# First block's operand sums made in later blocks from reloaded quadrants, six raw weight tiles at the start, a later slot for the key maxima, and later reuse of seven rooms

## The chip, the cores and the metric

The kernel runs on one core of a Trainium2 chip. The metric is device time in microseconds of one execution. Three runs of the kernel before gave 1580.91, 1583.93 and 1583.86 us, a median of 1583.86 us. The profiled execution is another one and took 1588.23 us.

## What is computed

Inputs `q`, `k`, `v` have 8 batches, 8 heads, 576 positions and 64 features. `q` is turned into a softmax over the features, `k` into a softmax over the positions. Then, for each batch and head, `kv = k_s^T v` (64 x 64) and `x = q_s kv`, and the heads are laid side by side: `x` is 4608 x 512. Two two-layer networks follow:

```python
h = x @ w_in          # 512 -> 2048
g = relu(h) ** 2
x = g @ w_out         # 2048 -> 512
h2 = x @ w_in2        # 512 -> 2048
g2 = h2 * sigmoid(h2)
out = g2 @ w_out2     # 2048 -> 512
```

The four weight matrices are handed over as 64-bit floats.

## The kernel before, in words

**Precision.** A matmul operand is split into a high part that TensorE takes at its fast rate and a low part; each product is three matmuls, high by high, high by low and low by high. So every weight and every activation costs a cast on ACT and a subtraction on DVE.

**Weights.** A weight tile comes as pairs of 32-bit words (`raw_load`, L166, 512 KB, a tile `wraw`). `rounding` (L198) makes 32-bit floats of it: a copy of the low words on ACT and three operations on DVE (`wu`). `w1_split` (L245) then makes `wh` on ACT and `wl` on DVE. The 16 tiles of the first layer (`wlist`, L1013) use three buffers, `doubles` (L118). The first three loads stand among the loads of the first inputs (`first_loads`, L1020); the other 13 are issued in the first seven slots of block 0, each when a buffer is free (L1117 to L1124).

**First stage.** The tokens are taken in nine blocks of 512 (L1096). A block has 16 slots; in slot t the matmul group `layer_in` (L673, 12 matmuls into bank `h`) makes 128 hidden features for the block's 512 tokens, and `hidden` (L694) squares the positive part on ACT into a tile `gs`. The attention of the next block is spread over the same slots: the table `ORDER` (L727) gives each step (`kv_max`, `kv_tr`, `kv_red`, `kv_diag`, `kv_bc`, `kv_sub`, `kv_exp`, `kv_mm`, ...) its slot, and `at` (L723) files it. From block 1 on every engine runs its instructions in the order of the program (`pinned`, L1099); in block 0 the compiler's scheduler chooses the order.

**Quadrants.** The later layers multiply 2 x 2 block matrices with seven products instead of eight. That needs, besides the four quadrants A11, A12, A21, A22 of an activation, the sums S1 to S4, where S3 takes the place of A21. In the first stage `g_first` (L705) makes S1 and S3 on DVE, `g_second` (L710) makes S2 and S4 on POOL, and `g_store` (L715) writes all seven slots of 128 x 256 to DRAM (`g1d`, 896 KB) from POOL's queue. A pair j of hidden tiles is written in slots 2j and 2j+1, summed in slots 2j+3 and 2j+4 and stored in slot 2j+5. `g_place` (L690) gives each pair one of six places: three tiles of 7 x 512, of which two are the tiles `st` of `stpool` and the third lies in `gpool`.

**After the first stage.** Steps (L771) take products one after another. Each step needs a pair `al`, `ah` of the activation (`a_load` on SP's queue 14 steps ahead, L778, `a_split` six steps ahead, L791) and a split weight (`product_weights`, L334). All of these live in rooms of 128 x 512 (`room`, L122), taken from the front of the queue `rooms` and given back at its end. When the first stage ends, `gpool` is closed, a pool `rpool` takes its bytes and 13 rooms are appended (L1143 to L1145). The two tiles `st` become slots for results, from which `hidden_after` (L864) takes its first two, `c11`, after the eighth step.

Of the kernel before, what the change touches and what calls it, by code (L numbers as in the profile page):

```python
# [10 lines left out]
I32 = mybir.dt.int32  # L11
# [14 lines left out]
def kernel(  # L26
# [36 lines left out]
    class InOrder:  # L63
# [16 lines left out]
    ve, ac, gp, sp, pe = (  # L80
        InOrder(e) for e in (nc.vector, nc.scalar, nc.gpsimd, nc.sync, nc.tensor)
    )
    P = 128
# [4 lines left out]
    TB = P * R  # L88
    HB = TB // 2
    NB = NT // TB  # L90
    KC = DM // P
    NF = DFF // P
    NG = NF // 2
# [20 lines left out]
    NU = 76  # L114

    rooms, banks, a_banks = deque(range(NU)), deque((0, 1, 6)), deque((2, 3, 4, 5, 7))
    lent, rpool = {}, []
    doubles = deque(range(3))  # L118
    g_pool_was = tc.tile_pool(name="gpool", bufs=1)
    g_pool = g_pool_was.__enter__()  # L120

    def room(dt=F32, name="u"):  # L122
        n = rooms.popleft()
        t = (upool if n < NU else rpool[0]).tile([P, TB], dt, tag=f"u{n}", name=name)
        lent[id(t)] = (t, n, rooms)
        return t
# [7 lines left out]
    def back(*ts):  # L134
        for t in ts:
            _, n, whence = lent.pop(id(t))
            whence.append(n)
# [14 lines left out]
    g1d = [dpool.tile([P, 7, NB * HB], F32, name=f"g1d{j}") for j in range(NG)]  # L152
    wd = {(ph, f): dpool.tile([P, DM], F32, name=f"wd{ph}_{f}") for ph in (1, 2, 3) for f in range(NF)}

    S2, S1, A21, A11, A22, A12, S4 = range(7)
    S3 = A21

    PRODUCTS = (
# [7 lines left out]
    def raw_load(ph, f):  # L166

        if ph < 2:
            n = doubles.popleft()
            t = g_pool.tile([P, 2 * TB], I32, tag=f"d{n}", name="wraw")  # L170
            lent[id(t)] = (t, n, doubles)
            if ph:
                src = w_out[ph].bitcast(I32)[f * P:(f + 1) * P, :]
            else:
                src = w_in[ph].bitcast(I32)[:, 2 * f * P:2 * (f + 1) * P].rearrange(
                    "(c p) f -> p c f", p=P
                )
            sp.dma_start(out=t if ph else t.rearrange("p (c f) -> p c f", c=KC), in_=src)
            return [t]
        got = []  # L180
        for h in range(2):
            t = room(I32, "wraw")
            if ph in w_in:
                sp.dma_start(
                    out=t.rearrange("p (c f) -> p c f", c=2),
                    in_=w_in[ph].bitcast(I32)[
                        2 * h * P:2 * (h + 1) * P, 2 * f * P:2 * (f + 1) * P
                    ].rearrange("(c p) f -> p c f", p=P),
                )
            else:  # L190
                sp.dma_start(
                    out=t,
                    in_=w_out[ph].bitcast(I32)[f * P:(f + 1) * P, h * TB:(h + 1) * TB],
                )
            got.append(t)
        return got
# [42 lines left out]
    def w1_load(x):  # L239
        raw1[x] = raw_load(*x)  # L240

    def w1_round(x):
        raw1[x] = rounded(x[0], raw1[x])
# [443 lines left out]
    g_tiles = [stpool.tile([P, 7, TB], F32, tag="st", name="gs") for _ in range(2)]  # L687
    g_tiles.append(g_pool.tile([P, 7, TB], F32, tag="gs", name="gs"))

    def g_place(i, j):  # L690
        n = i * NG + j
        return g_tiles[n // 2 % 3][:, :, n % 2 * HB:(n % 2 + 1) * HB]

    def hidden(i, f, h):  # L694
# [18 lines left out]
        gp.tensor_tensor(t[:, S4], t[:, A12], t[:, S2], op=ALU.subtract)  # L713

    def g_store(i, j):  # L715
        gp.dma_start(
            out=g1d[j][:, :, i * HB:(i + 1) * HB], in_=g_place(i, j)
        )


    side = {}

    def at(i, slot, fn, *a):  # L723
        i, slot = divmod(max(0, i * NF + slot), NF)
        side.setdefault((i, slot), []).append((fn, a))

    ORDER = (  # L727
        (x_mm, 12), (kv_mm, 4), (kv_tr, 0), (kv_red, 1), (q_out, 6), (q_back, 8),
        (kv_load, -5), (q_load, -3), (v_load, 0),
        (kv_max, -1), (kv_sub, 2), (kv_exp, 3), (kv_rc, 5),  # L730
        (kv_scale, 6), (kv_lo, 7), (q_max, 1), (q_sub, 2), (q_exp, 3), (q_norm, 4), (q_tr, 5),
        (q_hi, 10), (q_lo, 11), (x_hi, 13), (x_lo, 14), (kv_diag, 1), (kv_bc, 1),
    )
    OF_KV = (kv_load, v_load, kv_max, kv_tr, kv_bc, kv_diag, kv_red, kv_sub, kv_exp, kv_mm, kv_rc, kv_scale, kv_lo)
    for i in range(NB):
        for j in range(NG):
            at(i, 2 * j + 3, g_first, i, j)
            at(i, 2 * j + 4, g_second, i, j)
            at(i, 2 * j + 5, g_store, i, j)
    early = []  # L740
    for fn, d in ORDER:
        for nxt in range(1, NB):
# [270 lines left out]
    wlist = [(0, f) for f in FS]  # L1013
# [3 lines left out]
        qmax=q_max, qsub=q_sub, qexp=q_exp, qnorm=q_norm, qtr=q_tr, qout=q_out, qhi=q_hi, qlo=q_lo, kvmm=kv_mm,  # L1017
        rc=kv_rc, scale=kv_scale, xmm=x_mm, xhi=x_hi, xlo=x_lo, round=w1_round, split=w1_split,
    )
    first_loads = "q0 v0 w0 q1 k1 v1 q2 k2 v2 w1 q3 k3 v3 w2".split()  # L1020
    whole = "kmax kred qmax qsub qexp ksub kexp qnorm kvmm qtr qout rc scale qhi qlo xmm xhi xlo".split()
    first_steps = [f"{x}{j}" for j in range(KC) for x in whole]
    for x, before in (("round0", "qnorm0"), ("split0", "rc0"), ("round1", "kmax3"), ("split1", "kvmm3")):
# [39 lines left out]
    def go_on():  # L1063

        doing[:] = [x for x in doing if next(x, 0) != 0]
# [26 lines left out]
    nl = sum(what[0] == "w" for what in first_loads)  # L1092
# [3 lines left out]
    for n in range(NB * NF + 6):  # L1096
        i, t = divmod(n, NF)
        ends = i >= NB - 1
        pinned[0] = i > 0  # L1099
        if n == (NB - 1) * NF:  # L1100
            assert nw == len(w2list)
            back(kv_room, *kv_rooms, *kvf_rooms.values())
            todo = [(5, lambda g=g: raw_weights(1, g)) for g in range(NG)]
            todo += [
                (NG if m in (3, 2, 1, 5) else 0, lambda m=m: product_weights(1, m)) for m in FIRST_USE
            ]
        last = hs
        if n < NB * NF:
            f = FS[t]
            hs = i, f, layer_in(i, f)  # L1110
            if ends:
                back(wh1.pop((0, f)), wl1.pop((0, f)))
        else:
            hs = None
        if last:
            hidden(*last)
        for _ in range(2):  # L1117
            if i == 0 and nr < len(wlist):
                if nl < len(wlist):
                    w1_load(wlist[nl])  # L1120
                    nl += 1
                w1_round(wlist[nr])
                w1_split(wlist[nr])
                nr += 1  # L1124
        for fn, a in side.pop((i, t), ()):
            fn(*a)
        if not ends:
            go_on()
            if n >= 33 and nw < len(w2list) and t in (1, 4, 7):
                doing.append(round_to_dram(*w2list[nw]))  # L1130
                next(doing[-1])
                nw += 1
        elif n < NB * NF:
            if t >= 9:
                stream(2 * t - 32)
                stream(2 * t - 31)
            for _ in range(3):
                spare = 2 + AHEAD + SPLIT - held_by(1) - 2 * (NF - 1 - t)
                while todo and len(doing) < 6 and len(rooms) - owed[0] >= todo[0][0] + max(0, spare):
                    begin()  # L1140
                go_on()
    assert not side
    g_pool_was.__exit__(None, None, None)  # L1143
    rpool.append(ctx.enter_context(tc.tile_pool(name="rpool", bufs=1)))
    rooms.extend(range(NU, NU + 13))  # L1145
    banks.extend(a_banks)

    st.update({e: stpool.tile([P, 7, TB], F32, tag="st", name="st") for e in range(2)})
# [6 lines left out]
    ROUNDS |= {(2, u, x) for u in range(NS - 1) for x in (14, 24, 34)}  # L1155
    for n, (ph, u, x, j, done) in enumerate(steps):
        into = n % SUPER
        if into == 0:
            if done and ph == 1:
                todo += [(8, lambda g=g: seven(2, g)) for g in range(NG)]  # L1160
                todo[4:4] = [(4, lambda m=m: factor(0, m)) for m in FIRST_USE]
            if done and ph == 2:
                todo += [(5, lambda g=g: raw_weights(3, g)) for g in range(NG)]
                todo += [
                    (NG if m in (3, 2, 1, 5) else 0, lambda m=m: product_weights(3, m))
                    for m in FIRST_USE[:5] + (6, 5)
                ]
            if ph == 3 and u == ORDER3[0]:
                back(extra)
        if ph == 2 and not done and (x, j) == (0, NG - 2):  # L1170
            todo += [(4, lambda m=m, u=u: factor(u + 1, m)) for m in FIRST_USE]
        if w3list and (ph, u, into) in ROUNDS:
            doing.append(round_to_dram(*w3list.pop(0)))
            next(doing[-1])
        if ph == 2:
            catch_up(lambda: (2, j, x) in W and ready((2, u, x, 0)) and ready((2, u, x, 1)))
        else:
            catch_up(lambda: (ph, j, x) in W)
        stream(n)
        step(ph, u, x, j, done)  # L1180
        go_on()
        if ph == 2:
            spare = 2 if done else 0
        else:
            left = sum(m[0] == ph for m in steps[n + 1:n + 1 + AHEAD])
            spare = 2 + left + min(left, SPLIT) - held_by(ph)
        many = 7 if ph == 2 and not done else 5 if ph == 1 and done else 2
        while todo and len(doing) < many and len(rooms) - owed[0] >= todo[0][0] + spare:
            begin()
# [33 lines left out]
```

## Time and profile before

| What | us |
|---|---|
| Median of three runs | 1583.86 |
| Profiled execution | 1588.23 |
| Its span, first to last instruction | 1586.5 |
| TensorE (PE) busy | 1538.9 |
| VectorE (DVE) busy | 1122.5 |
| ScalarE (ACT) busy | 907.5 |
| GpSimd (POOL) busy | 622.0 |

All lines of the kernel's instructions are L73, a helper that records every operation, so instructions are told apart by the names of their tiles. The profiled execution lies 4.4 us above the median; its span leaves 1.7 us outside.

### The profile page before, as it was taken

The numbers are of one execution on the slowest core, as the hardware profiler recorded it, in microseconds if no ns is written. First come the engines' busy times: TensorE is split into PE (matmuls) and PEld (weight loads), VectorE is DVE, ScalarE is ACT, GpSimd is POOL, SyncE is SP. The second block draws the span as 40 slices with busy tenths as digits, with TensorE's granted clock in tenths as the row PEclk, the third lists the DMA queues.
The fourth block names the chain that finished last, engine by engine and source line by source line (L and its number), as shares of the span: only waits on it lengthen the run. The fifth ranks groups of instructions, "written<-read, shape, count | busy, mean of one in ns | idle before, by whom it ended". The sixth has DMA issues, their size and how long they took to land.

```text
span 1586.5 us, 25384 instructions
## 1 busy us (share of the span) xinstructions
PE 1538.9 (97%) x7676; PEld 1332.5 (84%) x7676; DVE 1122.5 (71%) x2260; ACT 907.5 (57%) x1926; POOL 622.0 (39%) x1009
## 2 busy tenths in 40 slices
PE   5979999999999899999999999999999999999998
PEld 3758888888888799999988999999988899888997
DVE  7996778887626876777698866766666965655654
ACT  6856666666545755455567554645555845444441
POOL 1054455555548210202042744444467140606150
PEclk9989999999999999999999999999999999999999
DMA  9668899998867788989897687778789786867682
GB/s 251 198 216 253 290 289 288 298 297 266 269 223 226 269 274 297 310 282 326 275 335 245 226 298 255 273 246 300 261 300 317 259 246 198 249 190 235 190 275 47
DMA packets 264713, 410.15 MB, mean 259 GB/s; under 512 B 70272, under 2 KB 199296, under 8 KB 264576
## 3 DMA queue, kind: packets, MB, share of 16 engines
q1 hardware_dynamic: 210896, 238.23, 49.0%
q0 software_dynamic: 50272, 168.86, 29.7%
q10 hardware_dynamic: 3408, 1.44, 0.4%
q8 instruction: 60, 0.98, 0.3%
q14 instruction: 77, 0.63, 0.1%
HBM read 230.42 MB, written 178.00 MB: 257 GB/s over the span
## 4 chain that ended last, share of the span: by engine, by line
PE 89%; DVE 3%; DMA 3%; POOL 2%; ACT 1%; issue 1%; SPq 0%; ACTq 0%; POOLq 0%; DVEq 0%
PE x L73 35%; PE h L73 23%; PE d L73 18%; PE a L73 9%; PE kvps L73 2%; PE xps L73 2%; POOL g2d L73 1%; POOL wt L73 1%; DMA al<-x2d 1%; DMA kr<-in_k_dram 1%; DVE xr L73 1%; DVE wu L73 1%; DMA wraw<-in_moe_w_in_dram 1%; DVE wl L73 0%; DMA g1d<-gs 0%
## 5 line engine op out<-in xcount | busy, mean ns | idle before, releaser
L73 DVE TENSOR_TENSOR al<-al,ah 128x448 fp32r<-128x448 f32 (+1 forms) x630 | 374.2, 642 | 188.0 <-ACT ah L73 183.6
L73 ACT CAST ah<-al 128x448 fp32r<-128x448 f32 (+1 forms) x630 | 334.4, 577 | 141.7 <-PE x L73 55.5
L73 PE MATMUL h<-x,wh 128*128 128x512 f32 x1152 | 369.3, 401 | 2.1 <-DVE x L73 1.8
L73 PE MATMUL x<-ah,wT 128*128 128x448 f32 (+1 forms) x960 | 288.4, 371 | 0.5 <-ACT st L73 0.5
L73 PEld LDWEIGHTS h<-x,wh 128*128 128x128 f32 x1152 | 216.1, 191 | 46.7 <-DVE x L73 2.0
L73 ACT COPY st<-x 128x448 f32<-128x448 f32 (+1 forms) x181 | 97.8, 543 | 251.0 <-PE x L73 236.0
L73 PE MATMUL h<-x,wl 128*128 128x512 f32 x576 | 227.3, 395 | 0.0
L73 PEld LDWEIGHTS x<-ah,wT 128*128 128x128 f32 x960 | 180.3, 188 | 21.7 <-ACT st L73 1.6
L73 POOL DMA_DIRECT2D g2d<-st x262 | 140.6, 541 | 131.5 <-ACT st L73 72.7
L73 PE MATMUL x<-al,wT 128*128 128x448 f32 (+1 forms) x480 | 178.0, 371 | 0.0
L73 POOL TENSOR_TENSOR gs<-gs 128x256 f32<-128x256 f32 x144 | 125.6, 872 | 131.5 <-DVE gs L73 102.7
L73 POOL DMA_DIRECT2D out_dram<-st x176 | 92.2, 533 | 195.8 <-DVE st L73 190.1
L73 ACT ACTIVATE gs<-h 128x512 f32<-128x512 f32 x144 | 85.8, 596 | 134.8 <-PE h L73 131.0
L73 PE MATMUL a<-ah,wB 128*128 128x448 f32 (+1 forms) x480 | 148.8, 371 | 0.0
L73 PE MATMUL d<-ah,wT 128*128 128x448 f32 (+1 forms) x480 | 145.3, 374 | 3.4 <-ACT ah L73 3.4
L73 PE MATMUL d<-ah,wB 128*128 128x448 f32 (+1 forms) x480 | 144.1, 371 | 0.0
L73 PE MATMUL x<-ah,wN 128*128 128x448 f32 (+1 forms) x480 | 143.9, 371 | 0.0
L73 PE MATMUL x<-ah,wB 128*128 128x448 f32 (+1 forms) x480 | 143.9, 371 | 0.0
L73 PEld LDWEIGHTS h<-x,wl 128*128 128x128 f32 x576 | 109.4, 190 | 24.0 <-DVE wu L73 0.2
L73 DVE TENSOR_TENSOR st<-st 128x448 f32<-128x448 f32 (+1 forms) x161 | 100.2, 648 | 26.6 <-ACT st L73 23.0
L73 PEld LDWEIGHTS d<-ah,wT 128*128 128x128 f32 x480 | 91.0, 190 | 13.7 <-issue 3.8
L73 PEld LDWEIGHTS d<-ah,wB 128*128 128x128 f32 x480 | 90.1, 188 | 10.3 <-DVE st L73 0.3
(124 smaller groups left out, 2678.9 us busy)
## 6 DMA issues: line engine op xcount, KB each, us to landing
g1d<-gs POOLq DMA_DIRECT2D x72, 896.0 KB, 5.6
al<-g1d SPq DMA_DIRECT2D x224, 224.0 KB, 4.1
al<-g2d SPq DMA_DIRECT2D x224, 224.0 KB, 3.1
g2d<-st POOLq DMA_DIRECT2D x210, 224.0 KB, 3.4
al<-g1d SPq DMA_DIRECT2D x56, 256.0 KB, 4.1
al<-g2d SPq DMA_DIRECT2D x56, 256.0 KB, 3.0
g2d<-st POOLq DMA_DIRECT2D x52, 256.0 KB, 3.9
al<-x2d SPq DMA_DIRECT2D x56, 224.0 KB, 5.4
```

The lines of the kernel that those rows point to most:

```text
L73: got = fn(*a, **kw)
```

## The change

The sums of block 0 are taken out of block 0: there `g_store` writes the four quadrants alone, two slots earlier. Each of the eight pairs is loaded again in a later block (`g_again`, `AGAIN`), summed there and its four sums are stored; blocks 1, 2, 3, 5, 6 and 7 take one pair each and block 4 takes two. The order of slots is changed so that the four sums and the four quadrants are each contiguous. Three more raw weight tiles lie in the third tile `gs` until the stage needs it (`views`; each is used twice), and three more loads stand at the end of `first_loads`, while `w1` stands ahead of the loads of head pair 2. `kv_bc`, `kv_sub`, `kv_exp`, `kv_mm`, `kv_rc`, `kv_scale` and `kv_lo` are one slot later. Of the 13 rooms, six are appended at the end of the first stage and seven at step 12. With eight more turns, the last two pairs of the stage lie in a tile `st` instead of the tile in `gpool`.

```diff
-    doubles = deque(range(3))
+    doubles, views = deque((-1, -2, -3, 0, 1, 2)), [0] * 3
...
-    S2, S1, A21, A11, A22, A12, S4 = range(7)
+    S4, S2, S1, A21, A11, A22, A12 = range(7)
...
             n = doubles.popleft()
-            t = g_pool.tile([P, 2 * TB], I32, tag=f"d{n}", name="wraw")
-            lent[id(t)] = (t, n, doubles)
+            if n < 0:
+                t = g_tiles[2].rearrange("p s c -> p (s c)").bitcast(I32)[:, 2 * TB * ~n:2 * TB * -n]
+                lent[id(t)] = (t, n, doubles if views else [])
+                views[:1] = []
+            else:
+                t = g_pool.tile([P, 2 * TB], I32, tag=f"d{n}", name="wraw")
+                lent[id(t)] = (t, n, doubles)
...
+    AGAIN = {(i, 3): i - 1 for i in (1, 2, 3, 5, 6, 7)} | {(4, 1): 3, (4, 5): 7}
+    turns = []
+    for i in range(NB):
+        for j in range(NG):
+            turns.append((i, j))
+            if (i, j) in AGAIN:
+                turns.append(AGAIN[i, j])
     def g_place(i, j):
-        n = i * NG + j
+        n = turns.index(j if i is None else (i, j))
...
     def g_store(i, j):
+        o = slice(A21, 7) if i == 0 else slice(0, A21 + 1) if i is None else slice(0, 7)
+        b = i or 0
         gp.dma_start(
-            out=g1d[j][:, :, i * HB:(i + 1) * HB], in_=g_place(i, j)
+            out=g1d[j][:, o, b * HB:(b + 1) * HB], in_=g_place(i, j)[:, o]
         )
+    def g_again(j):
+        sp.dma_start(out=g_place(None, j)[:, A21:7], in_=g1d[j][:, A21:7, 0:HB])
...
-        (x_mm, 12), (kv_mm, 4), (kv_tr, 0), (kv_red, 1), (q_out, 6), (q_back, 8),
+        (x_mm, 12), (kv_mm, 5), (kv_bc, 2), (kv_tr, 0), (kv_red, 1), (q_out, 6), (q_back, 8),
...
-        (kv_max, -1), (kv_sub, 2), (kv_exp, 3), (kv_rc, 5),
-        (kv_scale, 6), (kv_lo, 7), (q_max, 1), (q_sub, 2), (q_exp, 3), (q_norm, 4), (q_tr, 5),
-        (q_hi, 10), (q_lo, 11), (x_hi, 13), (x_lo, 14), (kv_diag, 1), (kv_bc, 1),
+        (kv_max, -1), (kv_sub, 3), (kv_exp, 4), (kv_rc, 6),
+        (kv_scale, 7), (kv_lo, 8), (q_max, 1), (q_sub, 2), (q_exp, 3), (q_norm, 4), (q_tr, 5),
+        (q_hi, 10), (q_lo, 11), (x_hi, 13), (x_lo, 14), (kv_diag, 1),
...
-            at(i, 2 * j + 3, g_first, i, j)
-            at(i, 2 * j + 4, g_second, i, j)
-            at(i, 2 * j + 5, g_store, i, j)
+            if i:
+                at(i, 2 * j + 3, g_first, i, j)
+                at(i, 2 * j + 4, g_second, i, j)
+            at(i, 2 * j + (5 if i else 3), g_store, i, j)
+            if (i, j) in AGAIN:
+                again = AGAIN[i, j]
+                at(i, 2 * j + 2, g_again, again)
+                at(i, 2 * j + 5, g_first, None, again)
+                at(i, 2 * j + 6, g_second, None, again)
+                at(i, 2 * j + 7, g_store, None, again)
...
-    first_loads = "q0 v0 w0 q1 k1 v1 q2 k2 v2 w1 q3 k3 v3 w2".split()
+    first_loads = "q0 v0 w0 q1 k1 v1 w1 q2 k2 v2 q3 k3 v3 w2 w3 w4 w5".split()
...
-                if nl < len(wlist):
+                if nl < len(wlist) and doubles:
...
-    rooms.extend(range(NU, NU + 13))
+    rooms.extend(range(NU + 7, NU + 13))
...
+        if n == 12:
+            rooms.extend(range(NU, NU + 7))
```

## Rows read from the trace of the kernel before

**Rows 1.** The page: the span, and busy time of each engine.

```profile
span 1586.5 us, 25384 instructions
PE 1538.9 (97%) x7676; PEld 1332.5 (84%) x7676; DVE 1122.5 (71%) x2260; ACT 907.5 (57%) x1926; POOL 622.0 (39%) x1009
```

**Rows 2.** The chain that ended last, first stage: start, length, what.

```profile
72.75 8.07 DMA wraw<-in_moe_w_in_dram
...
148.76 8.21 PE h L73 x36
...
161.64 8.21 PE h L73 x36
```

**Rows 3.** By stretch, blocks 4 and 5: PE, PEld, DVE, ACT, POOL, clock, DMA, GB/s.

```profile
269.50:321.00 51.50, 51.50 (x297) 41.78 (x297) 41.59 (x98) 35.03 (x72) 27.49 (x41) 1.00 0.93 297
...
324.00:337.00 13.00, 13.00 (x76) 10.54 (x75) 9.79 (x24) 8.94 (x18) 6.53 (x10) 1.00 1.02 328
```

**Rows 4.** By stretch, tile `h` alone: PE, PEld, ACT, clock, DMA, GB/s.

```profile
0.00:47.00 47.00, 8.71 (x24) 4.50 (x24) 0.00 (x0) 1.00 0.87 214
0.00:118.50 118.50, 59.21 (x205) 39.83 (x206) 9.93 (x17) 0.94 0.78 221
```

**Rows 5.** Busy time by stretch, 20 to 120 us (columns as in rows 3).

```profile
20.00:40.00 20.00, 17.04 (x104) 10.49 (x103) 15.83 (x43) 14.57 (x51) 0.87 (x1) 1.00 1.01 244
40.00:60.00 20.00, 17.08 (x134) 13.12 (x134) 18.25 (x46) 19.70 (x59) 0.29 (x3) 0.91 0.40 121
...
80.00:100.00 20.00, 15.79 (x74) 11.65 (x74) 17.46 (x35) 13.47 (x26) 8.93 (x13) 0.91 0.51 156
100.00:120.00 20.00, 13.61 (x78) 9.53 (x79) 19.45 (x49) 10.10 (x23) 12.82 (x19) 0.79 0.84 271
```

**Rows 6.** Waits of SP's queue, 0 to 125 us: total, times, longest.

```profile
SPq L73 <- DVE wu L73: 37.2, 11, 9.8
```

**Rows 7.** The end of the first stage in the timeline: ACT, PE, POOL.

```profile
531.86 0.40 ACT L73 CAST wT<-wt 128x256 fp32r<-128x256 f32 x1 [10.99 <-DMA g1d<-gs]
...
536.95 0.52 ACT L73 COPY st<-x 128x448 f32<-128x448 f32 x1
...
532.83 0.44 PE L73 MATMUL d<-ah,wT 128*128 128x448 f32 x1 [3.43 <-ACT ah L73]
...
519.98 0.91 POOL L73 DMA_DIRECT2D g1d<-gs  x1 [0.30 <-DVE wT L73]
```

**Rows 8.** The chain that ended last, around the end of the first stage.

```profile
525.98 5.78 DMA g1d<-gs
...
533.44 10.24 PE d L73 x41
...
583.37 9.92 PE d L73 x48
```

**Rows 9.** DVE's groups by form, 47 to 118 us: busy, mean ns, idle before.

```profile
L73 DVE TENSOR_TENSOR wl<-wu,wh 128x512 fp32r<-128x512 f32 x14 | 11.4, 819 | 2.0 <-ACT wh L73 1.9
...
L73 DVE TENSOR_TENSOR gs<-gs 128x256 f32<-128x256 f32 x16 | 7.7, 481 | 0.0
L73 DVE TENSOR_TENSOR xr<-q,sm 128x256 f32<-128x256 f32 x6 | 5.0, 869 | 0.0
L73 DVE TENSOR_SCALAR wu<-wraw 128x512 int32<-128x512 int32 x12 | 4.9, 417 | 2.5 <-DMA wraw<-in_moe_w_in_dram 2.5
```

**Rows 10.** DVE's groups by form, 125 to 460 us.

```profile
L73 DVE TENSOR_TENSOR xr<-q,sm 128x256 f32<-128x256 f32 x50 | 19.0, 421 | 0.9
...
L73 DVE TENSOR_TENSOR x<-xps,x 128x512 fp32r<-128x512 f32 x26 | 17.8, 683 | 4.6 <-ACT x L73 4.6
```

**Rows 11.** The timeline: load and first use of block 1's first keys.

```profile
15.45 1.42 SPq L73 DMA_DIRECT2D k<-in_k_dram  x1
...
31.89 0.41 DVE L73 TENSOR_TENSOR xr<-k 128x256 f32<-128x256 f32 x1
```

**Rows 12.** Waits, 20 to 125 us: PE for the broadcast of the key maxima.

```profile
PE kvps L73 <- ACT kvx L73: 5.0, 3, 2.0
```

## The prediction, made before the result was known

> **What bounds the kernel now.** I read the page first: PE is busy 1538.9 of 1586.5 us [rows 1], so 47.6 us of idle PE is the first thing to look for, together with stretches where PE is busy but slow. The chain of waits then shows what PE's own pace is in the first stage: the same pattern of 48 matmuls of tile h and one head pair's attention starts at 148.76 and again at 161.64 us [rows 2], which is 12.88 us for four slots, 3.22 us a slot, 51.5 us a block. In block 4 PE is busy 51.50 of 51.50 us, with DVE at 41.59 and POOL at 27.49 [rows 3]: from block 1's second slot to block 8 PE sets the pace and the other engines have room.
>
> It isn't so before that. By 118.5 us 205 matmuls of h are done, 24 of them by 47 us [rows 4]. At PE's pace the other 181 take 181 / 48 x 12.88 = 48.6 us; they took 71.5. So 23 us are lost between 47 and 118.5 us, and no more than that can be won there by feeding PE better. The busy times by stretch name the feeder: DVE is busy 18.25, 17.46 and 19.45 us of three stretches of 20 [rows 5]. The reader is to see two more things in these rows: the DMA share falls to 0.40 and 0.51 in two of them, though raw weights are still to come, and the granted clock is 0.91, 0.91 and 0.79 where PE has gaps, so part of the remaining matmuls run at 1.2 instead of 2.4 GHz. SP's queue says why DMA rests: it waited 37.2 us for DVE to free a raw buffer [rows 6]. Then one load, issued at 72.75, stands 8.07 us in the chain [rows 2].
>
> The third place is the end of the first stage. ACT idles 10.99 us for the last store of a tile `gs`, PE 3.43 us for ACT behind it [rows 7], and 41 matmuls after it take 10.24 us where 48 take 9.92 later on [rows 8].
>
> **The change, part by part.** (a) *DVE sums leave block 0.* 16 adds, 7.7 us in this stretch [rows 9]. From DVE's load between 47 and 118 that is all gain; at the 421 ns that the same size takes later [rows 10] it is 6.7, if what slowed them would slow another instruction instead.
>
> (b) *POOL sums leave block 0.* The stretch shows DVE operations slower than the same forms later: `xr<-q,sm` 869 ns against 421 six times, and `wl` 819 against 683 for an operation of its size 14 times [rows 9, 10]. That is 6 x 0.448 + 14 x 0.136 = 4.6 us of stretched DVE time. POOL's subtraction of the query maxima stays, and so do its store issues, so I take 3 (bounds 0 and 4.6). The Trainium skill, SBUF — State Buffer, "SBUF: two separate sides", says that VectorE and GpSimd share one port pair as an exclusive lock for a whole instruction, so that the later one blocks fully. By that DVE could stand still for as long as POOL works, 8.93 + 12.82 = 21.7 us between 80 and 120 us [rows 5], and the term would be near that instead of 3; the rows stretch by 4.6 in all, so the trace bears out the direction and not the full price.
>
> (c) *Six raw tiles.* The load ahead of a rounding grows from one tile to four, so the late loads should vanish: DVE's 2.5 us for the transfer and 1.9 us behind ACT's cast, which waits for the same load [rows 9]. I take 4 (bounds 0, and the 8.07 us of the chain).
>
> Together (a) to (c) take 7.7 + 3 + 4 = 14.7 us from DVE. PE's floor above allows 23. But the chain is not DVE alone between 47 and 118: for part of it PE or ACT is last (ACT is busy 19.70 of 20 between 40 and 60 [rows 5]). I take two thirds, **10 us**; bounds 3 and 16.
>
> (d) *Loads at the start.* DMA is full between 20 and 40 us, at 244 GB/s [rows 5]. Three more tiles of 0.52 MB in front of block 1's loads delay these by 1.57 / 0.244 = 6.4 us, and `w1` delays head pair 2 by 2 us. Block 1's first keys are issued at 15.45 and first used at 31.89 [rows 11], so most of that is covered; if that cover is short, DVE starts late. I charge **1 us** (bounds 0 and 6).
>
> (e) *Key maxima a slot later.* PE waited 5.0 us in three pieces for the broadcast, all in the DVE-bound part [rows 12]; 3.22 us more lead would cover each (longest 2.0). These waits lie inside the 23 us counted above, so I add nothing (bounds 0 and 3). Later PE has no idle time that it could give back [rows 3].
>
> (f) *What blocks 1 to 7 get.* Per pair: a load and a store of 0.52 MB, two adds on DVE, two subtractions and an issue on POOL, one issue on SP. DVE has 10 us spare in block 4 and POOL 24 [rows 3]; an add is 0.42 to 0.48 us. The reload is issued three slots, 9.7 us, ahead of its add, behind whatever SP waits for; if it is late DVE waits in order, and with it the casts behind it. A place is now overwritten after five slots where it was seven, in block 4 once after three, 9.7 us, against 5.78 us for a store to land [rows 8]. DMA share in block 4 is 0.93 at 297 GB/s [rows 3], so 319 GB/s at full share; two pairs there are 2.1 MB, 6.6 us of 51.5, which makes 1.06. The overrun of 3 us has to find room in the lead of the transfers. I charge **1 us** (bounds 0 and 6).
>
> (g) *Rooms and the last tile.* The last pairs now end in a tile `st`, and the tile in `gpool` is last read by the store issued at 519.98 [rows 7]. With 5.78 us to land [rows 8] its bytes are free at 525.8 instead of 531.8. Whether the six rooms lie on those bytes the trace doesn't show; I assume that they do, so ACT goes on at 525.8, six us earlier. PE's step needs its cast at 529.4 and gets it: 3.4 us saved. The 41 matmuls lose their slow start, 10.24 - 41 x 9.92 / 48 = 1.8 us. What is late next is `c11`: its copy at 536.95 comes 5.1 us after ACT resumes [rows 7], so about 531, and its slot is freed by the very last store at 531.8. That is a wait of 1 us on ACT with PE six steps ahead. **5 us** (bounds 0 and 7).
>
> Sum: 10 - 1 + 0 - 1 + 5 = 13 us. On the profiled execution's 1588.2 that is 1575; the runs' median lies 4.4 us lower at 1583.9, so the forecast there is **1571 us**.
>
> **The rivals.** *Only the end is won.* In block 0 the scheduler may order DVE, ACT and PE so that the freed DVE time turns into idle time behind PE or ACT, or the start is pushed by (d) as far as the middle wins. For it: ACT's 19.70 of 20. Against: in the last 20 us before PE takes over DVE is the fullest engine at 19.45, PE at 13.61 and ACT at 10.10 [rows 5]. Then 5 - 1 = 4 us remain: 1580.
>
> *The room edit does nothing.* The bytes or the `st` slot hold ACT as long as before. Then 8 us remain: 1576.
>
> *Slower: DMA becomes the bound in blocks 2 to 6.* Eight loads and eight stores are 8.4 MB, at 319 GB/s 26 us. If queues are in effect full at 0.93, each of these us stops PE through late keys, queries and places, and 1584 - 13 + 26 = 1597. It decides from the point where a block's share passes 1.0 before the change's own 0.06 a pair. Against: PE is busy 13 of 13 us at a share of 1.02 and 328 GB/s [rows 3]. The Trainium skill, DMA: Bandwidth & Descriptors, "Issuing engines are not separate DMA queues", says that transfers started from SP and POOL run on the same 16 engines and interleave. By that rule the reloads on SP's queue get no bandwidth of their own next to POOL's stores, which speaks for this rival; the share of 1.02 without a PE wait speaks for its mildest form, a few us.
>
> *Nothing measurable.* (d) and (f) at their upper bounds eat the gain: 10 + 5 - 6 - 6 = 3 us, 1581.
>
> **How the numbers follow.** Forecast, 1571, with its sizes: 0.55. Only the end, 1580: 0.15. Room edit idle, 1576: 0.10. Nothing measurable, 1581 to 1586: 0.12. Slower, up to 1597: 0.08. A measurement of this kernel can tell about 0.2%, 3.2 us, from no change. Faster by more than that is the forecast, the room rival and most of the second: 0.79; within it 0.13; slower 0.08. For the range the lower end takes (a) to (c) at 16, (g) at 7 and no charges, 23 us: 1561. The upper end takes in the second rival and the edge of the fourth: 1582.
>
> **What would show it.** Right: no `gs` add on DVE in block 0 and none of its waits for `wraw`; 205 matmuls of h done near 108 us instead of 118.5; the clock near 1.00 in 100 to 120; PE still without idle time in block 4 at a share near 1.0; ACT's wait for the store of `gs` ended by 526 and PE busy over 9 us of the stretch from 530 to 540. Wrong: DVE still fullest up to 118 with as many instructions done, ACT or PE last in its place, block 1's keys late, PE idle time between 125 and 460, or ACT waiting at `c11` so long that PE runs out of splits.

## The result, and the profile of the changed kernel

The changed kernel takes 1569.3 us (median of four runs, 1566.6 to 1571.4) against 1583.9 before: ratio 0.991, 95% interval 0.9887 to 0.9933, so 10.6 to 17.9 us faster. The profiled execution took 1571.4 us with a span of 1569.6, 16.8 us less than the span before.

The page of the changed kernel: PE is busy 4 us less and idle 13 us less than before [rows 1].

```profile
span 1569.6 us, 25423 instructions
...
PE 1534.9 (98%) x7676; PEld 1327.8 (85%) x7676; DVE 1122.9 (72%) x2260; ACT 906.5 (58%) x1926; POOL 625.4 (40%) x1017
```

Busy time by stretch, changed kernel, 20 to 120 us and then block 4 (columns as in rows 3):

```profile
20.00:40.00 20.00, 18.27 (x110) 11.92 (x111) 16.35 (x45) 15.69 (x47) 0.81 (x1) 0.91 0.98 272
40.00:60.00 20.00, 16.87 (x121) 13.16 (x120) 18.43 (x48) 19.39 (x64) 2.11 (x5) 0.91 0.86 233
...
80.00:100.00 20.00, 19.84 (x116) 14.74 (x117) 19.77 (x48) 15.47 (x33) 6.30 (x12) 1.00 0.54 162
100.00:120.00 20.00, 19.27 (x101) 14.94 (x99) 15.32 (x39) 13.54 (x29) 7.77 (x11) 1.00 0.67 195
...
256.50:308.40 51.90, 51.90 (x297) 41.79 (x297) 44.75 (x101) 34.86 (x71) 30.57 (x47) 1.00 1.00 327
```

Against [rows 5], little has moved up to 60 us (matmul 60 of `h` starts at 57.6 us instead of 60.3), and much between 80 and 120: PE goes from 15.79 and 13.61 to 19.84 and 19.27 us, the clock from 0.91 and 0.79 to 1.00, and DVE is no longer full in the last stretch. Block 4 carries the added bytes at a share of 1.00, where it was 0.93 [rows 3], with no idle PE.

Tile `h` alone, changed kernel (columns as in rows 4):

```profile
0.00:104.00 104.00, 56.80 (x204) 38.14 (x204) 10.13 (x17) 0.97 0.83 230
...
0.00:118.50 118.50, 69.79 (x257) 47.98 (x258) 12.53 (x21) 0.97 0.82 228
```

204 matmuls are done by 104 us, where 205 had taken 118.5 [rows 4].

DVE's groups, 47 to 118 us, changed kernel (columns as in rows 9):

```profile
L73 DVE TENSOR_TENSOR wl<-wu,wh 128x512 fp32r<-128x512 f32 x13 | 8.7, 685 | 3.3 <-ACT wh L73 3.3
...
L73 DVE TENSOR_TENSOR xr<-q,sm 128x256 f32<-128x256 f32 x8 | 4.3, 575 | 0.1
...
L73 DVE TENSOR_SCALAR wu<-wraw 128x512 int32<-128x512 int32 x8 | 3.3, 420 | 1.5 <-DMA wraw<-in_moe_w_in_dram 1.5
```

Both forms are shorter than in [rows 9]: 685 ns where 819 stood, and 575 where 869 stood. Of the 16 adds of `gs` 4 remain, block 1's. With six raw tiles DVE still waits 1.5 us for a raw load, where it was 2.5; the prediction had named the end of these waits as a sign of being right.

The end of the first stage in the timeline of the changed kernel: POOL's stores of the pairs (8, 5) and (8, 7), PE, ACT.

```profile
507.98 0.90 POOL L73 DMA_DIRECT2D g1d<-gs  x1 [0.30 <-DVE wT L73]
513.14 0.48 PE L73 MATMUL x<-al,wB 128*128 128x448 f32 x1 [2.26 <-DVE al L73]
513.97 0.90 POOL L73 DMA_DIRECT2D g1d<-gs  x1 [0.30 <-POOL gs L73]
514.98 0.41 ACT L73 CAST wT<-wt 128x256 fp32r<-128x256 f32 x1 [6.54 <-DMA g1d<-gs]
```

ACT waits 6.54 us instead of 10.99, and goes on 7.0 us after the store of pair (8, 5) was issued, not after the last one. PE's 3.43 us [rows 7] are gone; its 2.26 us for DVE's `al` are a wait that stood there before too, with 1.64 us.

The chain in blocks 1 and 2 of the changed kernel shows the one loss: the pattern that repeated after 12.88 us [rows 2] now repeats after 12.97, with PE never waiting.

```profile
150.15 5.49 PE h L73 x24
...
163.12 5.49 PE h L73 x24
```

### The profile page after: what moved, and what is told of

Same layout as the page of the kernel before. It is cut to its first block, busy times and chain, and to the rows that moved or that the text cites. A ratio compares the mean times of both kernels' runs of the same rounds, so it can differ in the third digit from the quotient of the medians.

```text
span 1569.6 us, 25423 instructions
## 1 busy us (share of the span) xinstructions
PE 1534.9 (98%) x7676; PEld 1327.8 (85%) x7676; DVE 1122.9 (72%) x2260; ACT 906.5 (58%) x1926; POOL 625.4 (40%) x1017
## 4 chain that ended last, share of the span: by engine, by line
PE 91%; DVE 3%; ACT 2%; DMA 1%; POOL 1%; issue 1%; ACTq 0%; SPq 0%; DVEq 0%; POOLq 0%
PE x L73 37%; PE h L73 22%; PE d L73 19%; PE a L73 10%; PE kvps L73 2%; PE xps L73 2%; POOL wt L73 1%; DVE wT L73 1%; DVE al L73 1%; ACT q L73 0%; DVE xr L73 0%; DVE st L73 0%; DMA wraw<-in_moe_w_in_dram 0%; DMA k<-in_k_dram 0%; DMA g1d<-gs 0%
## 5 line engine op out<-in xcount | busy, mean ns | idle before, releaser
L73 PEld LDWEIGHTS h<-x,wh 128*128 128x128 f32 x1152 | 211.3, 189 | 48.6 <-ACT x L73 2.1
L73 PEld LDWEIGHTS x<-al,wT 128*128 128x128 f32 x480 | 90.1, 188 | 10.2
```

The costliest lines, as they stand in the source:

```text
L73: got = fn(*a, **kw)
```

## The experiments

Three marks are counted in every trace: when matmul 240 of `h` starts (just behind block 1's start; all counts begin with 0), the time from there to matmul 1200 (blocks 1 to 6), and the time from matmul 0 of the second stage to matmul 75 (its slow start). Before they are 128.3, 257.60 and 23.3 us; changed 113.8, 259.47 and 18.3.

| run | median us | ratio, 95% interval | start of 240 | 240 to 1200 | first 75 |
|---|---|---|---|---|---|
| old key slots in the changed kernel | 1570.1 | 0.9893 to 0.9937 | 116.4 | 258.64 | 18.8 |
| new key slots alone | 1585.0 | 0.9995 to 1.0022 | 124.0 | 259.47 | 24.4 |
| raw tiles alone | 1581.1 | 0.9966 to 0.9996 | 126.8 | 257.60 | 23.6 |
| sums alone | 1569.6 | 0.9886 to 0.9926 | 113.4 | 258.34 | 18.3 |
| turns alone | 1577.8 | 0.9946 to 0.9986 | 128.1 | 257.60 | 18.0 |
| changed, rooms at once | 1568.5 | 0.9869 to 0.9933 | 111.5 | 259.49 | 18.3 |
| sums, `gs` after loads | 1567.7 | 0.9867 to 0.9930 | 115.4 | 258.31 | 19.5 |
| sums, new slots in block 1 | 1567.1 | 0.9863 to 0.9932 | 116.9 | 258.63 | 19.3 |
| changed, two pools | 1567.0 | 0.9874 to 0.9913 | 115.5 | 259.47 | 19.0 |
| two pools, new slots in block 1 | 1566.8 | 0.9874 to 0.9917 | 112.2 | 258.59 | 19.1 |
| subtractions on DVE | 1580.0 | 0.9965 to 0.9993 | 124.5 | 257.60 | 23.8 |
| changed, more bytes | 1575.0 | 0.9912 to 0.9960 | 113.9 | 267.95 | 19.5 |

How far the first mark scatters by itself: the changed kernel, its versions with rooms at once, with two pools and with more bytes issue the same matmuls up to it, and start matmul 240 at 113.8, 111.5, 115.5 and 113.9. Differences under some 4 us there say nothing. The second mark repeats to 0.05 us. The ratios are to executions of the kernel before taken beside each run, whose medians are 1582.5 to 1584.0 us.

**One part at a time.** The first five runs take the keys out of the whole, and then each part alone.

```diff
-        (x_mm, 12), (kv_mm, 5), (kv_bc, 2), (kv_tr, 0), ...
+        (x_mm, 12), (kv_mm, 4), (kv_tr, 0), ...
-        (kv_max, -1), (kv_sub, 3), (kv_exp, 4), (kv_rc, 6),
+        (kv_max, -1), (kv_sub, 2), (kv_exp, 3), (kv_rc, 5),
...
+        ... (kv_diag, 1), (kv_bc, 1),
```

> The changed kernel with the key steps back in their old slots (only ORDER is undone). In the changed kernel matmuls of h lose 0.19 us per 96 between the 216th and the 1200th, 2.2 us in all, with no wait on PE. Theory A (the spread keys break the broadcast and the ten key-value matmuls out of one run of PE work, and each extra change of matmul kind costs PE time): 96 matmuls of h come 25.76 us apart again instead of 25.95, the whole is 2 us faster than the changed kernel, about 1567, if block 1 starts as early. Theory B (the loss is the reloads and extra sums): 96 matmuls of h still take 25.95 us, whole unchanged at 1569. Rival C (the spread is what removed the stall at the start of block 1, where 9.5 of the 16.9 us came from): PE waits for the broadcast again, 5 us in three pieces as before, and the whole is 3 to 9 us slower than the changed kernel, 1572 to 1578.

The second mark falls from 259.47 to 258.64, not to 257.60: the slots cost what theory A says, and PE waits elsewhere (below). The whole is level with the changed kernel. Theory B, that the reloads slow PE, falls with the next run, which has no reloads and the same 259.47.

The reverse edit, on the kernel before:

> The kernel before with the key steps in their new slots, nothing else. Theory A: 96 matmuls of h go from 25.76 to 25.95 us from block 1 on, 2 us lost over the seven blocks; with DVE as full as before up to 118 us the start gains under 3 us, so 1583 to 1586. Theory B: 25.76 us stays. Rival C (the spread alone removes the stall at the start of block 1): 1574 to 1577.

The chain of this run, blocks 1 and 2:

```profile
147.30 5.49 PE h L73 x24
...
156.34 0.73 PE kvps L73 x20
...
160.28 5.49 PE h L73 x24
```

12.98 us a pattern. Where before it was 36 matmuls of `h` in one run [rows 2], it is 24. The key-value matmuls (ten in the program, 20 short ones in the trace) stood behind the `xps` products in one group of other work; now they have a place of their own, so that a head pair's other work interrupts the matmuls of `h` three times instead of twice. 0.09 us for each of 20 head pairs is the 1.86 us of the second mark. At the start 4.4 us are won, about what that mark scatters by, and the whole gains nothing (0.9995 to 1.0022).

The raw tiles and the order of the first loads, on the kernel before (the hunks at `doubles`, `raw_load`, `first_loads` and `and doubles`):

> The kernel before with six raw tiles at first and the new order of the first loads, nothing else. By the prediction's terms 4 us of DVE waits vanish at two thirds, less 1 us of later loads: 1.7 us faster, 1582 (bounds 1579 and 1590). Rival: the chain of the changed kernel still holds a raw load of 6.07 us where 8.07 stood, so the raw tiles only move the load: within 0.2% of before, 1581 to 1587.

0.6 to 5.4 us faster, where 1.7 was expected.

The sums, on the kernel before (the hunks at `S4`, `AGAIN`, `g_place`, `g_store`, `g_again` and `side`):

> The kernel before with the first block's sums made in later blocks from reloaded quadrants (its new slices of the operand tile and its new turns with it), with three raw tiles, the old slots of the keys and all 13 rooms at once. By the prediction's terms (a) and (b), 10.7 us of DVE at two thirds, 7 us, less 1 us in the later blocks; the last pair now ends in another tile, so the rooms come free as early as in the prediction's (g), up to 5 us more: 1573 to 1578. Rival (the spread or the raw tiles are needed before the freed DVE time reaches PE): 205 matmuls of h are done at 115 us or later instead of 108, and the whole is over 1579. Rival (the reloads cost in blocks 1 to 7): 96 matmuls of h take 25.9 us or more instead of 25.76.

This part by itself has the whole gain. (The new turns belong to it, so the last pairs of the stage lie in a tile `st` here too, and the third mark falls.) Its stretches (columns as in rows 3):

```profile
80.00:100.00 20.00, 19.37 (x117) 14.80 (x118) 18.86 (x49) 16.24 (x36) 6.36 (x13) 1.00 0.55 167
100.00:120.00 20.00, 19.30 (x118) 15.01 (x117) 15.45 (x40) 13.07 (x27) 7.04 (x10) 1.00 0.65 194
```

Its DVE groups, 47 to 118 us (columns as in rows 9):

```profile
L73 DVE TENSOR_TENSOR wl<-wu,wh 128x512 fp32r<-128x512 f32 x13 | 9.0, 689 | 3.3 <-ACT wh L73 3.1
...
L73 DVE TENSOR_SCALAR wu<-wraw 128x512 int32<-128x512 int32 x12 | 5.0, 419 | 0.0
```

DVE's 2.5 us of waiting for a raw load [rows 9] are gone with three raw tiles: the loads had been late because DVE freed their buffers late.

How the first gain divides can be read at a subtraction `ql` on DVE: the products `xps` between the matmuls 203 and 204 of `h` wait for it, and behind it the chain is PE's. It ends at 115.56 us before, at 103.64 in the changed kernel and at 103.34 with the sums alone. From the span's start to there, and from there to matmul 240 (columns as in rows 3; before, changed, sums alone, then before and changed):

```profile
0.00:115.56 115.56, 82.83 (x474) 58.77 (x474) 98.56 (x252) 80.97 (x222) 30.76 (x63) 0.95 0.78 219
0.00:103.64 103.64, 80.08 (x474) 57.52 (x474) 87.76 (x237) 80.13 (x221) 19.00 (x50) 0.97 0.83 229
0.00:103.34 103.34, 77.07 (x474) 55.47 (x474) 87.84 (x238) 81.18 (x222) 18.87 (x50) 0.98 0.80 227
...
115.50:128.30 12.80, 12.68 (x61) 10.06 (x62) 9.21 (x23) 6.39 (x14) 6.42 (x10) 0.76 0.94 285
...
103.60:113.80 10.20, 10.10 (x61) 8.12 (x62) 8.68 (x23) 6.09 (x13) 3.81 (x6) 1.00 0.67 198
```

With the sums alone `ql` ends 12.2 us earlier. DVE is busy 10.7 us less, with 14 instructions fewer: 14 adds, which are 5.9 us at 0.42 us each, and 4.8 us by which these and other operations had been lengthened. Its idle time is 1.5 us less. The other 2.7 us, to the 14.9 at matmul 240, are PE's clock: the same 61 matmuls behind `ql` take 12.80 us at a granted clock of 0.76 before, behind a gap of PE (part of them at 1.2 instead of 2.4 GHz), and 10.20 at 1.00 in the changed kernel.

In blocks 1 to 6 this kernel loses 0.74 us, of which its waits between 125 and 460 us show one piece (total, times, longest):

```profile
PE kvps L73 <- ACT kvx L73: 0.4, 1, 0.4
```

It is in block 4: DVE works almost without a gap from the reloaded pair's two adds to a maximum of the keys two slots later, and comes to that maximum 1.8 us later than before, counted from the same matmul. The head pair with this wait takes 0.65 us longer. The new slots cover this wait, and cost 1.86 us to do so.

**The end of the stage.** First the turns of the operand tiles alone, on the kernel before:

```diff
-        n = i * NG + j
+        n = i * NG + j + 2
```

> The kernel before with the turns of the three operand tiles shifted by one, so that the last pairs end in a tile st and the tile in gpool is last read by the store of pair (8, 5); all 13 rooms at once, nothing else. Theory (the prediction's (g), with the six early rooms of no weight): ACT's wait for the store of gs goes from 10.99 to about 6 us, PE's 3.4 us behind it and the slow matmuls after it vanish, 5 us in all: 1579. Rival (the split of the rooms is what counts): ACT waits for the very last store as before, 1584.

5.4 us faster by the ratio 0.9966 (2.2 to 8.6), and 5.35 us in the third mark (23.33 to 17.98).

```profile
525.27 0.47 PE L73 MATMUL x<-al,wB 128*128 128x448 f32 x1 [1.97 <-DVE al L73]
...
526.27 0.41 ACT L73 CAST wT<-wt 128x256 fp32r<-128x256 f32 x1 [5.59 <-DMA g1d<-gs]
```

The split of the rooms, taken back in the changed kernel:

```diff
-    rooms.extend(range(NU + 7, NU + 13))
+    rooms.extend(range(NU, NU + 13))
...
-        if n == 12:
-            rooms.extend(range(NU, NU + 7))
```

> The changed kernel with all 13 rooms given at once, as in the kernel before. Theory (the split of the rooms does nothing, the new turns did it): ACT's wait stays at 6 to 7 us, time within 0.2% of the changed kernel's 1569. Rival (the split counts): PE waits 3 us behind ACT at the end of the first stage, 1573 to 1574.

No difference that can be told, and the third mark is the same 18.3 us. The split does nothing.

Then the places of the bytes, in the kernel with the sums alone:

```diff
-    g_tiles.append(g_pool.tile([P, 7, TB], F32, tag="gs", name="gs"))
...
     for what in first_loads:
         run(what)
+    g_tiles.append(g_pool.tile([P, 7, TB], F32, tag="gs", name="gs"))
```

> The kernel with the sums alone (old keys, three raw tiles, 13 rooms at once), and the operand tile in gpool requested after the first loads, so that the raw tiles come first in gpool and the six first rooms of the next stage lie on their bytes, free since block 7. Theory: ACT's wait of 6.07 us for the store of gs goes, and PE's waits of 2.24 and 0.26 us for DVE's al behind it: 2 to 3 us faster than the sums alone, 1567. Rival (the bytes are not given in order of request, or the slots of st hold ACT next): no change, 1569 to 1570.

ACT's wait is as long as before:

```profile
514.50 0.41 ACT L73 CAST wT<-wt 128x256 fp32r<-128x256 f32 x1 [5.86 <-DVE wT L73]
```

The addresses that the program was given do put the six first rooms on the raw tiles' bytes, and the instruction is the same one, ACT's first write to a new room. So it waits for the closed pool as a whole, not for the bytes under its own room. (DVE is named as the releaser; but the write also waits for the semaphores of the stores of the pairs (8, 4) and (8, 5), and the later of these landed at 514.40 us, 0.1 us before it.) Two pools in place of one put that to the test:

```diff
+    pools_were = [tc.tile_pool(name=x, bufs=1) for x in ("gpool", "gspool")]
+    g_pool, gs_pool = (x.__enter__() for x in pools_were)
...
+        t = (upool if n < NU else rpool[n >= NU + 6]).tile(...)
...
+    for x in reversed(pools_were):
+        x.__exit__(None, None, None)
+    rpool.extend(ctx.enter_context(tc.tile_pool(name=x, bufs=1)) for x in ("rpool", "rspool"))
```

> The changed kernel with the raw tiles and the operand tile in two pools: gpool holds the three raw tiles, a second one the tile gs; when both are closed, six rooms are opened on the first and seven on the second, all 13 given at once. Theory (the rooms' first write waits for the last reader of the closed pool as a whole, which is why it stayed at 6 us when the raw tiles were put under the first rooms): ACT does the casts into the six rooms at once and waits for the store of gs five casts later; PE's waits of 2.26 and 0.24 us for DVE's al vanish, 2.5 us less than the changed kernel: 1567 (1566 to 1568). Rival (ACT runs into the wait anyway before PE has what it needs): no change, 1568 to 1570.

DVE, POOL, PE and ACT in this kernel's timeline:

```profile
512.62 1.79 DVE L73 TENSOR_TENSOR al<-al,ah 128x448 fp32r<-128x448 f32 x1
513.04 1.96 POOL L73 TENSOR_TENSOR gs<-gs 128x256 f32<-128x256 f32 x2
514.46 0.47 PE L73 MATMUL x<-al,wB 128*128 128x448 f32 x1 [1.91 <-DVE al L73]
515.54 0.61 DVE L73 TENSOR_TENSOR al<-al,ah 128x448 fp32r<-128x448 f32 x1
516.37 0.57 ACT L73 CAST ah<-al 128x448 fp32r<-128x448 f32 x1 [5.06 <-DMA g1d<-gs]
```

ACT now writes into the rooms and stops later, at a cast of `ah`: the pool as a whole was what it had waited for. PE's time hardly changes, though, as the rival said: its 1.91 us end while ACT still waits, so ACT wasn't their cause. The subtraction that PE waits for takes 1.79 us beside POOL's sums, and 0.61 when POOL is quiet.

**Keys in block 1 only.** On the sums alone, and then on two pools:

```diff
-    for fn, d in ORDER:
-        for nxt in range(1, NB):
+    for fn, d, blocks in [(*x, (1,)) for x in SPREAD] + [(*x, range(2, NB)) for x in ORDER]:
+        for nxt in blocks:
```

> The kernel with the sums alone, and the new key slots for block 1's heads only; blocks 2 to 7 keep the old ones. Theory (the spread wins at the start of block 1 and costs 0.19 us per two head pairs later): the 216th matmul of h starts 1 to 3 us earlier than with the sums alone (107.87), 96 matmuls of h take 25.76 us, and the whole is 1 to 3 us faster, 1567 to 1569. Rival (with DVE freed by the moved sums nothing waits for block 1's keys any more): 216th matmul at 107 to 108.5, whole within 1 us.

> The kernel with two pools, and the new key slots for block 1's heads only, blocks 2 to 7 with the old ones. Theory: the 2.2 us that the new slots cost from block 1 to 6 come back, less some 1 us of PE waiting for the broadcast of the keys behind the extra sums, as with the old slots in two runs: 1 us less than with two pools alone, 1566, and 96 matmuls of h 25.76 us apart. Rival (the old slots let PE wait for the broadcast at each of the eight extra pairs, 0.4 us and more each): 1567 to 1570.

Neither stands out. Matmul 240 starts at 116.9 and 112.2, inside the scatter; the second mark is 258.6, so 0.9 of 1.86 us come back, and the old slots' own loss of 1.0 us takes the rest, 0.65 of it at the wait for the broadcast in block 4. The last kernel has the lowest median here, 1566.8, but its interval holds the ratios of all versions that move the sums and add no bytes.

**POOL beside DVE.** The prediction's terms (a) and (b) come apart when the first block's subtractions go to DVE and its adds stay:

```diff
-        gp.tensor_tensor(t[:, S2], t[:, S1], t[:, A11], op=ALU.subtract)
-        gp.tensor_tensor(t[:, S4], t[:, A12], t[:, S2], op=ALU.subtract)
+        on = gp if i else ve
+        on.tensor_tensor(t[:, S2], t[:, S1], t[:, A11], op=ALU.subtract)
+        on.tensor_tensor(t[:, S4], t[:, A12], t[:, S2], op=ALU.subtract)
```

> The kernel before with the two subtractions of each of the first block's pairs on DVE instead of POOL, nothing else: 16 operations of 481 ns more on DVE, 7.7 us, and none of them on POOL. By the rows (POOL's sums stretch DVE's operations by 4.6 us in all) DVE gets 3.1 us fuller: 0 to 3 us slower, 1584 to 1587. By the rule of an exclusive lock for the whole of each POOL instruction DVE would get back up to 21.7 us less 7.7: 14 us at two thirds, 9 us faster, 1575.

1.1 to 5.5 us faster, with more work on DVE. Its groups between 47 and 118 us (columns as in rows 9):

```profile
L73 DVE TENSOR_TENSOR gs<-gs 128x256 f32<-128x256 f32 x31 | 13.6, 439 | 0.1
L73 DVE TENSOR_TENSOR wl<-wu,wh 128x512 fp32r<-128x512 f32 x13 | 8.9, 688 | 1.8 <-ACT wh L73 1.7
...
L73 DVE TENSOR_TENSOR xr<-q,sm 128x256 f32<-128x256 f32 x6 | 2.3, 418 | 0.0
```

`xr<-q,sm` is back at 418 ns: its 869 came from POOL's subtractions. One such place in the kernel before:

```profile
107.33 1.76 POOL L73 TENSOR_TENSOR gs<-gs 128x256 f32<-128x256 f32 x2 [1.10 <-DVE sm L73]
107.55 1.82 DVE L73 TENSOR_TENSOR xr<-q,sm 128x256 f32<-128x256 f32 x2
```

Two operations of 0.42 us take 1.82 while POOL's two subtractions last 1.76. The Trainium skill, SBUF — State Buffer, "SBUF: two separate sides", says that a DVE operation with two SBUF inputs and a GpSimd operation that reads SBUF exclude each other for a whole instruction. The trace agrees at such places. As a price for POOL's whole busy time the rule gave 9 us here, and 1.1 to 5.5 were measured.

These 1.1 to 5.5 us are not the price of POOL's work by itself, because another wait comes last in this run. A stretch of it (columns as in rows 3), and its chain there:

```profile
100.00:110.00 10.00, 1.76 (x5) 0.98 (x5) 6.50 (x19) 3.39 (x9) 2.44 (x5) 0.67 0.69 236
```

```profile
95.59 2.38 DMA qd<-q
...
101.53 4.92 DMA xr<-qd
```

DVE is no longer full there; PE is nearly empty, behind a bounce of queries through DRAM. By DVE's own account up to `ql`, which ends at 112.36 us here, it is busy 96.42 us (98.56 before) with 12 adds and subtractions of `gs` more, 5.0 us at 0.42: some 7 us of lengthening are gone with POOL's subtractions.

**More bytes.** Behind each reload, in the changed kernel:

```diff
         sp.dma_start(out=g_place(None, j)[:, A21:7], in_=g1d[j][:, A21:7, 0:HB])
+        for x in range(2):
+            sp.dma_start(out=spare[j, x], in_=g1d[j][:, A21:7, 0:HB])
```

> The changed kernel with two more copies of the same 0.52 MB behind each reload, from the quadrants in DRAM to a place in DRAM that nobody reads, on SP's queue: 16 copies, 8.4 MB, as much again as all reloads and stores that the change adds. Theory (DMA has room in blocks 1 to 7, late transfers are taken up by their lead): PE stays without waits between 110 and 450 us, no more than 2 us slower than the changed kernel, 1569 to 1571. Rival (the slower case of the prediction, one step on: a share near 1 means that added bytes stop PE): 8.4 MB at 319 GB/s, up to 26 us, 1580 to 1595, with PE waiting for keys, queries or places in block 4 first.

The profiled execution, 1583.4 us, is the slowest of the six (the others took 1567.3 to 1577.4), so it shows what can happen and not how often. PE takes the bytes without a wait up to 330 us and then waits three times in 15 us, 5.0 us together; 8.7 us are lost between the matmuls 1008 and 1104 of `h`, in block 5. The chain there:

```profile
323.18 8.74 DMA qd<-q
...
334.67 3.44 DMA xr<-qd
...
343.31 3.42 issue
```

The stretches before and behind it (columns as in rows 3):

```profile
275.00:300.00 25.00, 25.00 (x146) 20.11 (x145) 23.94 (x51) 17.30 (x35) 14.15 (x22) 1.00 1.06 356
...
345.00:355.00 10.00, 8.28 (x43) 6.84 (x44) 9.66 (x19) 6.49 (x14) 7.33 (x9) 0.66 1.10 362
```

In block 4 the share was 1.06 at 356 GB/s and PE full. A store of the queries' bounce through DRAM then took 8.74 us, SP stood behind it, and queries, keys and PE followed, with part of the stretch at half clock. But this store is not slow for this kernel alone: the changed kernel's store of the same queries took 7.96 us, and PE didn't wait. What differs is when it was issued. The queue of SP in the changed kernel:

```profile
292.62 3.21 SPq L73 DMA_DIRECT2D xr<-qd  x4
...
313.71 1.01 SPq L73 DMA_DIRECT2D qd<-q  x1
```

And with more bytes:

```profile
294.64 7.22 SPq L73 DMA_DIRECT2D xr<-qd  x4
...
323.18 0.44 SPq L73 DMA_DIRECT2D qd<-q  x1
```

The four loads at 294.64 us stand behind two added copies; they take 7.22 us to issue instead of 3.21, the first of them lands after 13.2 us, and the store two head pairs later is issued 9.5 us late. So the slower rival is a real mechanism, as lost lead of SP's queue: it can come with twice the bytes that the change adds in blocks 1 to 7, and the change's own bytes leave PE without a wait.

## Why the prediction was right

The forecast of 1571 us holds. In the profiled executions, 14.5 us are won by matmul 240, 1.9 lost from there to 1200, 5.1 won in the next stage's slow start, and 0.9 lost after it (last section): 16.8 where the sum had 13. That the total lies so near is in part luck: the first gain is 14.5 us where (a) to (d) had 9, and losses of 2.8 us that the sum did not have, against its charge of 1 us in (f), took part of it back.

**(a), (b)** name the right work, and are nearly the whole of the first gain. The sums alone start matmul 240 14.9 and 13.0 us earlier in two kernels that issue the same instructions; (a) and (b) had 10.7 at two thirds, 7. The sizes in full were near: up to `ql` 14 adds are 5.9 us, where (a) had 7.7 for 16, and the lengthening is 4.8, where (b) had 3: together the same 10.7. What was mis-sized is the share that reaches PE: the sum took two thirds, and all of it arrived. In the kernel before, the chain that ended last is made of DVE's operations from 86 to 115 us. And no term stood for PE's half clock behind the gap, 2.7 us. (b)'s 4.6 us in the rows were also misread in part: "819 against 683, 14 times" is two long operations, and the longer of them, 2.04 us at 86.39, ran beside POOL's subtraction of the query maxima, which the change leaves. The run with POOL's subtractions on DVE should have been up to 3 us slower by these rows, and was 1.1 to 5.5 faster: the lengthening by POOL was some 7 us and not 4.6.

**(c)** was right about the wait and wrong about its cause. It goes without the six tiles, because the loads had been late behind DVE, and with them 1.5 us of it stay in the changed kernel. Alone the tiles win 0.6 to 5.4 us; on top of the sums nothing that can be told from the scatter. **(d)**: no cost can be told from the scatter either.

**(e)** was put at nothing, "later PE has no idle time that it could give back". It can still lose time: the new slots put one more interruption between the matmuls of `h`, 0.09 us a head pair, 1.86 us. In return they cover the wait behind the extra sums, 0.7 to 1.0 us with the old slots.

**(f)** was charged 1 us and cost nothing: a share of 1.00 in block 4, no wait on PE. With the old key slots it would have cost the 0.7 to 1.0 us.

**(g)**, 5 us, measured 5.1, by half of its mechanism. The last pairs' tile did it, as the run with the turns alone shows. The six rooms had no part. The assumption that a room waits for the bytes under it was wrong: the first write waits for the closed pool. The rival "the room edit does nothing" was true of the edit and false of its price. The wait of 1 us at `c11` didn't come.

**Rivals.** DVE's freed time did reach PE, so "only the end" fell. The DMA rival is shown in one execution at three times the reloads.

## What to carry to other kernels

Work moved away from an engine is worth most at the place where that engine is last and another one starves; price it there, with what a neighbour's work adds to its operations, instead of by a share of the whole; and add what the starved engine's clock gives back. Before giving a step more lead on an engine that is always busy, look at how often it then interrupts the other work. And test a bundle part by part: here one part, with the turns that came with it, had the whole gain, and one gave some of it back.

## What had not been expected of the hardware

PE's pace itself differs between executions of the same matmuls. The stretch from 610 to 740 us, which no edit touches, in the kernel before and in that with two pools:

```profile
610.00:740.00 130.00, 130.00 (x631) 118.07 (x630) 97.58 (x201) 66.87 (x140) 20.86 (x39) 1.00 0.88 293
```

```profile
610.00:740.00 130.00, 130.00 (x644) 120.46 (x643) 100.22 (x208) 68.98 (x143) 21.51 (x40) 1.00 0.92 308
```

PE is busy throughout at full clock in both, and does 631 matmuls in one and 644 in the other. They start 206 to 208 ns apart in the first; in the second four gaps in five are 199 to 203. Stretches of either pace come in different places of each execution and are worth 1 us in 50. The 0.9 us that the profiled execution of the changed kernel lost late is mostly of this kind (some 600 matmuls around 1300 us fell 2.3 us behind, at 206 and 207 ns where the kernel before had 199 to 203 in part; up to there it had been 1.4 us ahead), and it may be part of why runs of one kernel differ by 5 to 10 us. What sets the pace is open.
